# Two more PSUM buffers for the results of the layers, once the last head's scores are done

## The chip, the cores and the metric

The program runs on one core of one Trainium2 chip. The metric is the device time of one execution in microseconds (us): the median of three runs was 1069.62 us, the runs lying between 1068.02 and 1071.15 us.

## The reference

Attention with a decay, over 8 batches of 8 heads, 576 positions and 64 channels, and behind it two dense layers with a hard swish between them, over all 4608 tokens. Everything is float32.

```python
# q, k, v: (8, 8, 576, 64); f: (8, 8, 576)
scores = scale * q @ k.T
cum    = cumsum(log(clip(f, 1e-4, 1)))
scores = where(causal, -1e9, scores + cum[..., :, None] - cum[..., None, :])
attn   = exp(scores - max); attn /= attn.sum(-1) + 1e-9
x      = (attn @ v) -> (4608, 512)
h      = x @ w_in            # 512 -> 2048
g      = h * clip(h + 3, 0, 6) / 6
out    = g @ w_out           # 2048 -> 512
```

## The kernel before

**The work.** The 64 heads go through one after another (the loop over `VH`): scores by matmul into PSUM, maximum, exponential, weights times values, and the result `xT` laid down by transposing DMAs. As soon as all the heads of a batch are through, the two layers of that batch are appended to the list `units`, and `fill` hands pieces of them to TensorE (PE) between the pieces of the next heads. Every number is carried as a high and a low half in 16 bits, so each product in the layers is three matmuls (lines 785 to 787 and 832 to 834).

**Results of the layers.** A result is one tile of 128 partitions by 512 floats in PSUM, summed up by many matmuls and then taken out:

- `h_unit` (first layer, tile `ph`): 12 matmuls over 512 columns, traced in two blocks of six. Taken out by ScalarE (ACT, L791, `Relu` into `r`), VectorE (DVE, L794, the product, which reads `ph` a last time), ACT again (L795, high half into `gT`) and DVE again (L796, low half into `gT`). There are 16 of these for a batch.
- `out_unit` (second layer, tile `po`): 48 matmuls in eight blocks of six, which read all of `gT` and `w2`. Taken out by one ACT instruction (L838) into `o`, which a DMA writes to memory (L841). There are four for a batch.
- `rest_unit` (tile `ph_r`) and `out_unit` with the name `r…` (tile `po_r`): the same for the 64 tokens of each batch that fill no group of 512, for two batches together. `rest_unit` has 48 matmuls over 128 columns, in two blocks of 24; L817 (twice, ACT), L821 (DVE), L823 (ACT) and L824 (DVE) take it out, into `g_end` for the last pair of batches (the profile calls that place `vst`). Four `rest_unit`s, one last `out_unit`.

`gT` exists once: the first layer of a batch may overwrite a part of it only when all four `out_unit`s of the batch before have read that part. `r` has three buffers, `o` two.

**PSUM.** Four pools: `ps_s` (tag `S`, two buffers of 1024 floats, the heads' scores, `pn` and `ps`), `ps_m` (tag `mm`, two buffers of 512), `ps_t` (tag `tr`, one of 512) and `ps_a` (one, weights times values). `mm_tile` deals out the buffers of the layers: it counts the results in `turn`, and where `three` is set every third result takes `tr`, the others `mm`. So three buffers turn. In all 196 results are dealt out; 166 of them are asked for before the line `done(prev[0])` behind the loop, 30 after it: the last result of the first layer of batch 6 (counting from 0), four `out_unit`s of batch 6, and for batch 7 sixteen `h_unit`s, four `rest_unit`s, four `out_unit`s and the last `po_r`.

**What sets the order.** The order on each engine is laid down when the program is built, by a planner that walks through the program on estimated times. Of the instructions of an engine whose inputs and buffer are there, it takes the one with the lowest trace number, and it settles some matmuls ahead of the running one. Buffers of one tag go to their requests in traced order. `fill` traces each block inside `tc.high_priority(offset=-LOW_M)` with `LOW_M = 0`: its numbers start from where the outer trace stands, and the outer trace does not advance. Behind the heads nothing else is traced, only

```python
    while units:
        fill(1)
```

so there all blocks start from the same number, and only the place inside the block counts. Two results whose buffers and inputs are there therefore take turns in blocks of six, and a `rest_unit`, with its blocks of 24, gives way from its seventh matmul on to every block of six that is ready. On the chip each engine then runs its list strictly in this order.

Of the kernel before, what the change touches and what calls it, by code (L numbers as in the profile page):

```python
# [11 lines left out]
F32 = mybir.dt.float32  # L12
# [8 lines left out]
def kernel(  # L21
# [12 lines left out]
    NHEAD, D, S = qk.shape  # L34
# [5 lines left out]
    P = 128  # L40
# [6 lines left out]
    TT = 512  # L47
# [7 lines left out]
    ps_s = ctx.enter_context(tc.tile_pool(name="ps_s", bufs=2, space=bass.MemoryType.PSUM))  # L55
# [694 lines left out]
    def x_move(v):  # L750

        kind, n = VH[v]
        g = n if kind == "A" else n // 2
        b, cc = divmod(g, NPAIR)
        xhl = xpair[g][1]
        c0, c1, rest = {"A": (0, CA, None), "B": (CA, NCH - 1, NCH - 1), "F": (1, NCH, 0)}[kind]
        o = c0 - (1 if kind == "F" else 0)
        if rest is not None:
            nc.sync.dma_start_transpose(
                xT[2][:, cc, b // 2, :, 64 * (b % 2):64 * (b % 2) + 64],  # L760
                xhl[0:64, rest].rearrange("p a e -> p (a e)"),
            )
        nc.sync.dma_start_transpose(
            xT[b % 2][:, cc, o:o + c1 - c0].rearrange("p c a t -> p (c a) t"),
            xhl[:, c0:c1].rearrange("p c a e -> p (c a e)"),
        )


    turn = [0]

    def mm_tile(name, three):

        turn[0] += 1
        if three and turn[0] % 3 == 0:
            return ps_t.tile([P, TT], F32, tag="tr", name=name)
        return ps_m.tile([P, TT], F32, tag="mm", name=name)

    def h_unit(x, fc, c0, c1, b, three, name):

        nw = c1 - c0  # L780
        ph = mm_tile(f"ph_{name}_{fc}_{c0}", three)[:, :nw]
        fs_ = slice(fc * P, (fc + 1) * P)
        for cc in range(NCC):
            xh, xl = (x[:, cc, c0 // P:c1 // P, hl] for hl in range(2))
            nc.tensor.matmul(ph, w1[0][:, cc, fs_], xh, start=(cc == 0), stop=False)  # L785
            nc.tensor.matmul(ph, w1[0][:, cc, fs_], xl, start=False, stop=False)  # L786
            nc.tensor.matmul(ph, w1[1][:, cc, fs_], xh, start=False, stop=(cc == NCC - 1))  # L787
            if cc == 1 and nw == TT:
                yield H_COST
        r = p2.tile([P, TT], F32, tag="rt", name=f"r_{name}_{fc}_{c0}", bufs=3)[:, :nw]  # L790
        nc.scalar.activation(  # L791
            r, ph, AF.Relu, bias=bias_r, scale=scol(A1 + NG * b + fc * NG // NFC)
        )
        nc.vector.scalar_tensor_tensor(r, r, 6.0 * CG, ph, op0=ALU.min, op1=ALU.mult)  # L794
        nc.scalar.copy(gT[:, 0, fc, c0:c1], r)  # L795
        nc.vector.tensor_tensor(gT[:, 1, fc, c0:c1], r, gT[:, 0, fc, c0:c1], op=ALU.subtract)  # L796
        yield H_COST

    def rest_unit(k, j, g):

        n = NFC // NG
        ph = mm_tile(f"ph_r{k}_{j}", True)
        for i in range(n):
            fs_ = slice((n * j + i) * P, (n * j + i + 1) * P)
            dst = ph[:, i * P:(i + 1) * P]
            for cc in range(NCC):
                xh, xl = (xT[2][:, cc, k, hl] for hl in range(2))
                nc.tensor.matmul(dst, w1[0][:, cc, fs_], xh, start=(cc == 0), stop=False)  # L808
                nc.tensor.matmul(dst, w1[0][:, cc, fs_], xl, start=False, stop=False)
                nc.tensor.matmul(dst, w1[1][:, cc, fs_], xh, start=False, stop=(cc == NCC - 1))  # L810
            if i == n // 2 - 1:
                yield H_COST
        r = p2.tile([P, TT], F32, tag="rt", name=f"r_r{k}_{j}", bufs=3)
        r3, p3 = (t.rearrange("p (f t) -> p f t", t=P) for t in (r, ph))
        for i in range(2):
            o = slice(64 * i, 64 * i + 64)
            nc.scalar.activation(  # L817
                r3[:, :, o], p3[:, :, o], AF.Relu, bias=bias_r,
                scale=scol(A1 + NG * (2 * k + i) + j),
            )  # L820
        nc.vector.scalar_tensor_tensor(r, r, 6.0 * CG, ph, op0=ALU.min, op1=ALU.mult)  # L821
        hi, lo = (g[:, hl, n * j:n * (j + 1), 0:P] for hl in range(2))
        nc.scalar.copy(hi, r3)  # L823
        nc.vector.tensor_tensor(lo, r3, hi, op=ALU.subtract)  # L824
        yield H_COST

    def out_unit(s, col, rows, three, name, g=gT):

        po = mm_tile(f"po_{name}_{s}", three)
        ts_ = slice(s * P, (s + 1) * P)  # L830
        for fc in range(NFC):
            nc.tensor.matmul(po, g[:, 0, fc, ts_], w2[:, fc, 0, :], start=(fc == 0), stop=False)  # L832
            nc.tensor.matmul(po, g[:, 0, fc, ts_], w2[:, fc, 1, :], start=False, stop=False)  # L833
            nc.tensor.matmul(po, g[:, 1, fc, ts_], w2[:, fc, 0, :], start=False, stop=(fc == NFC - 1))  # L834
            if fc % 2 and fc < NFC - 1:
                yield 2.0 - H_COST
        o = p2.tile([P, DM], F32, tag="o", name=f"o_{name}_{s}")
        nc.scalar.activation(o, po, AF.Copy, scale=scol(col))  # L838
        p = 0
        for r0, r1 in rows:  # L840
            nc.sync.dma_start(out[r0:r1, :], o[p:p + r1 - r0])  # L841
            p += r1 - r0
        yield 2.0 - H_COST

    def moe_in(b, c0=0, c1=TT):

        for fc in range(NFC):
            j, new = divmod(fc, NFC // NG)
            if new == 0 and c0 == 0:
                while j not in w_in_done:  # L850
                    next(w_in_q, None)
                moe_scale_in(b, j)
            yield from h_unit(xT[b % 2], fc, c0, c1, b, b > 0 or c0 > 0, f"{b}")

    def moe_out(b, c0=0, c1=TT):

        if b == 0:
            for _ in wq:
                pass
        if c0 == 0:  # L860
            moe_scale_out(b)
        for s in range(c0 // P, c1 // P):
            r = S * b + (64 if b else 0) + s * P
            yield from out_unit(s, UO + b, [(r, r + P)], b > 0 or s * P >= QA, f"{b}")
# [4 lines left out]
    def rest_in(k, g):  # L869

        for j in range(NG):
            yield from rest_unit(k, j, g)

    def rest_out(k, g):

        b = 2 * k
        r = S - 64 if b == 0 else S * b
        yield from out_unit(
            0, UX + b + 1, [(r, r + 64), (S * (b + 1), S * (b + 1) + 64)], True, f"r{k}", g
        )  # L880
# [52 lines left out]
    def fill(k):  # L933
        credit[0] += k * rates[0]
        while credit[0] >= 1 and units:
            with tc.high_priority(offset=-LOW_M):
                r = next(units[0], 0)
            if r == 0:
                units.pop(0)
            else:  # L940
                credit[0] -= r
        credit[0] = min(credit[0], 1.0)

    def done(v):
        kind, n = VH[v]
        if kind == "A":
            if n == NPAIR - 1:
                units.append(moe_in(0, 0, QA))
                units.append(moe_out(0, 0, QA))
            return  # L950
        b, h = divmod(n, H)
        if h == H - 1:
            cut = QA if b == 0 else 0
            units.append(moe_in(b, cut, TT))
            if b == B - 1:
                units.append(rest_in(b // 2, g_end))
            units.append(moe_out(b, cut, TT))
            if b == B - 1:
                units.append(rest_out(b // 2, g_end))
            elif b % 2:  # L960
                units.append(rest_in(b // 2, gT))
                units.append(rest_out(b // 2, gT))

    prev = None
    pend_x = None
    vq = v_scale(0)
    for i, (kind, n) in enumerate(VH):
# [61 lines left out]
        prev = (i, ph)  # L1029
# [2 lines left out]
    fill(4)  # L1032
    x_move(prev[0])
    done(prev[0])
    while units:
        fill(1)

# [35 lines left out]
```

## Time and profile before

| | |
|---|---|
| median of 3 runs | 1069.62 us (1068.02 to 1071.15) |
| the profiled execution | 1067.75 us, of which the profile's span is 1065.7 us |
| PE busy | 1005.6 us (94%), 7650 matmuls |
| DVE, ACT, POOL busy | 714.6, 633.5, 439.4 us |
| chain that ended last | PE 81%, DVE 9%, ACT 4%, DMA 4%, issue 2% |
| mean granted PE clock | 0.988 |

A row of the timeline gives start and length in us, engine, line, operation, `out<-in`, the shape and how many are merged (`x3`); in brackets stands how long the engine had been idle and what released it. [...] A row of the table by stretches gives, for a stretch of the span, the busy time of each engine (and its instructions), then the granted PE clock as a share, the share of DMA and GB/s. The waits are listed as "engine line waited for: us in total, times, longest".

### The profile page before, as it was taken

What the parts mean: (1) busy time and instruction counts of PE and PEld (TensorE: products, weight loads), DVE (VectorE), ACT (ScalarE), POOL (GpSimd) and SP (SyncE); (2) the same over time, 40 slices, a digit from 0 to 9 for tenths busy, and PEclk for the clock granted to TensorE, in tenths of its full rate; (3) what the DMA queues carried; (4) which work ended last, traced back from release to release, by engine and by line L of the source; (5) the groups of instructions that cost most, each with busy time, mean ns of one, the idle gap of its engine ahead of it and who ended that gap; (6) DMA issues with size and microseconds to landing.
All of it is one profiled execution on the core that took longest, in us unless ns stands there. A gap on an engine that the chain in (4) does not pass through costs nothing.

```text
span 1065.7 us, 21332 instructions
## 1 busy us (share of the span) xinstructions
PE 1005.6 (94%) x7650; PEld 598.6 (56%) x7650; DVE 714.6 (67%) x1887; ACT 633.5 (59%) x1257; POOL 439.4 (41%) x641
## 2 busy tenths in 40 slices
PE   2799967899999999999999999999999999999897
PEld 2567844665555755555555755555555755444543
DVE  6878799886867678866885778847895677115300
ACT  5798667766864657656755657646764666125301
POOL 9635556435544445454553445545544430000000
PEclk9999989999999999999999999999999999999999
DMA  8875446936766675567565755566556544010000
GB/s 239 275 216 174 110 101 136 210 77 118 158 118 120 119 160 106 95 144 154 104 125 109 160 112 109 106 130 163 105 97 137 91 89 74 12 40 1 1 20 30
DMA packets 253717, 123.83 MB, mean 116 GB/s; under 512 B 225860, under 2 KB 227452, under 8 KB 253612
## 3 DMA queue, kind: packets, MB, share of 16 engines
q1 hardware_dynamic: 253612, 122.47, 53.2%
q8 instruction: 60, 0.98, 0.4%
q14 instruction: 45, 0.37, 0.1%
HBM read 47.93 MB, written 9.73 MB: 54 GB/s over the span
## 4 chain that ended last, share of the span: by engine, by line
PE 81%; DVE 9%; ACT 4%; DMA 4%; issue 2%; SPq 0%; POOL 0%; ACTq 0%; DVEq 0%; POOLq 0%
PE ph L785 10%; PE ph L786 10%; PE ph L787 10%; PE po L832 10%; PE po L834 10%; PE po L833 10%; PE pn L622 3%; PE pn L619 3%; DMA ring<-in_w_in_dram 2%; DVE pp L630 1%; PE pav L706 1%; PE pav L707 1%; PE pav L705 1%; PE po_r L834 1%; PE ph_r L808 1%
## 5 line engine op out<-in xcount | busy, mean ns | idle before, releaser
L642 ACT ACTIVATE pp<-pp,nb 128x192 f32<-128x192 f32 x280 | 138.4, 552 | 133.7 <-DVE nb L636 119.6
L785 PE MATMUL ph<-xT,w 128*128 128x512 f16 (+1 forms) x576 | 198.4, 358 | 3.6 <-ACT o L838 2.3
L659 DVE TENSOR_TENSOR ring<-pp,ring 128x128 f16<-128x128 f32 (+2 forms) x216 | 142.2, 671 | 83.5 <-ACT ring L656 77.8
L787 PE MATMUL ph<-xT,w 128*128 128x512 f16 (+1 forms) x576 | 197.9, 357 | 0.0
L786 PE MATMUL ph<-xT,w 128*128 128x512 f16 (+1 forms) x576 | 197.8, 357 | 0.0
L832 PE MATMUL po<-w,gT 128*128 128x512 f16 x512 | 189.5, 381 | 7.5 <-ACT w L284 3.5
L833 PE MATMUL po<-w,gT 128*128 128x512 f16 x512 | 192.1, 381 | 3.7 <-DVE w L295 3.7
L464 POOL TENSOR_TENSOR T<-ST,TQ 64x288 fp32r<-64x288 f32 (+2 forms) x136 | 112.0, 825 | 199.2 <-PE pn L622 153.0
L834 PE MATMUL po<-w,gT 128*128 128x512 f16 x512 | 191.7, 381 | 0.0
L630 DVE CUSTOM_DVE_ANT_0 pp<-pn,W 128x192 f32<-128x192 f32 x280 | 123.5, 483 | 32.1 <-PE pn L622 21.9
L794 DVE SCALAR_TENSOR_TENSOR r<-r,ph 128x512 f32<-128x512 f32 (+1 forms) x144 | 89.1, 620 | 68.1 <-ACT r L791 67.5
L619 PE MATMUL pn<-TK,TQ 68*128 68x192 f32 x336 | 125.9, 388 | 5.8 <-issue 5.7
L469 POOL TENSOR_TENSOR T<-ST,T 64x288 fp32r<-64x288 f32 (+1 forms) x136 | 125.5, 941 | 12.6 <-ACT T L462 7.9
L791 ACT ACTIVATE r<-ph,bias_r,SC 128x512 f32<-128x512 f32 (+1 forms) x144 | 103.8, 725 | 26.0 <-PE ph L787 22.8
L796 DVE TENSOR_TENSOR gT<-r,gT 128x512 f16<-128x512 f32 (+1 forms) x144 | 102.5, 714 | 23.5 <-ACT gT L795 21.8
L622 PE MATMUL pn<-T,T 128*128 128x192 f32 x336 | 116.0, 370 | 0.0
L656 ACT CAST ring<-pp 128x192 f16<-128x192 f32 x280 | 114.4, 450 | 0.2
L795 ACT CAST gT<-r 128x512 f16<-128x512 f32 (+1 forms) x144 | 81.1, 566 | 40.6 <-DVE r L794 40.2
L665 POOL TENSOR_TENSOR ring<-pp,ring 128x128 f16<-128x128 f32 x96 | 56.1, 584 | 104.0 <-ACT ring L656 84.4
L834 PEld LDWEIGHTS <-gT 128*128 128x128 f16 x560 | 54.7, 98 | 70.0 <-issue 10.3
L833 PEld LDWEIGHTS <-gT 128*128 128x128 f16 x560 | 54.9, 98 | 65.1 <-issue 10.2
L787 PEld LDWEIGHTS <-w 128*128 128x128 f16 x576 | 56.5, 98 | 57.0 <-issue 6.6
(159 smaller groups left out, 2036.3 us busy)
## 6 DMA issues: line engine op xcount, KB each, us to landing
ST<-in_qk_dram SPq DMA_DIRECT2D x64, 288.0 KB
ring<-in_w_out_dram SPq DMA_DIRECT2D x16, 512.0 KB
out_dram<-o SPq DMA_DIRECT2D x32, 256.0 KB
T<-TQ SPq DMA_DIRECT2D x56, 144.0 KB
vst<-in_vS_dram SPq DMA_DIRECT2D x7, 1040.0 KB
ring<-in_w_in_dram SPq DMA_DIRECT2D x9, 512.0 KB
w<-in_w_in_dram SPq DMA_DIRECT2D x7, 512.0 KB
vst<-in_vS_dram SPq DMA_DIRECT2D x14, 130.0 KB
```

The source lines that it names most:

```text
L469: nc.gpsimd.tensor_tensor(T1[j][0:D, a:e], s[D:, a:e], T1[j][D:, a:e].bitcast(F32), op=ALU.subtract)
L619: nc.tensor.matmul(dst, TQ[i][0:D + 4, qs], TK[i][0:D + 4, a:e], start=True, stop=False)
L622: nc.tensor.matmul(dst, T7[j][:, qs], T1[j][:, a:e], start=False, stop=True)
L630: nc.vector.tensor_tensor_reduce(pp[:r, w:w + kw], pn[:r, o:o + kw], W[:r, 4 * P + r - kw:4 * P + r], 1.0, -3.0e38, ALU.add, ALU.max, accu ...
L642: nc.scalar.activation(x_, x_, AF.Exp, bias=nb[:r, e0 + x:e0 + x + 1], scale=0.125)
L659: eng.tensor_tensor(hl[:r, a:a + c * P], pp[:r, at[c] + 64:at[c] + kw], hl[:r, h0[c] + 64:h0[c] + kw], op=ALU.subtract,)
L785: nc.tensor.matmul(ph, w1[0][:, cc, fs_], xh, start=(cc == 0), stop=False)
L786: nc.tensor.matmul(ph, w1[0][:, cc, fs_], xl, start=False, stop=False)
L787: nc.tensor.matmul(ph, w1[1][:, cc, fs_], xh, start=False, stop=(cc == NCC - 1))
L832: nc.tensor.matmul(po, g[:, 0, fc, ts_], w2[:, fc, 0, :], start=(fc == 0), stop=False)
L833: nc.tensor.matmul(po, g[:, 0, fc, ts_], w2[:, fc, 1, :], start=False, stop=False)
L834: nc.tensor.matmul(po, g[:, 1, fc, ts_], w2[:, fc, 0, :], start=False, stop=(fc == NFC - 1))
```

## The change

From the point where the last head is through, `mm_tile` gives every result with an odd count a buffer of `ps_s` (half of it is used), and the results with an even count go on as before: `tr` where the count can be divided by three, `mm` otherwise. Of the 30 results after that point, those with the counts 167, 169, … 195 go to `S`: 15 of them. Two buffers of `S`, two of `mm` and one of `tr` make five. No instruction is added or taken away.

```diff
     turn = [0]
+    heads_done = []
 
     def mm_tile(name, three):
 
         turn[0] += 1
+        if heads_done and turn[0] % 2:
+            return ps_s.tile([P, 1024], F32, tag="S", name=name)[:, :TT]
         if three and turn[0] % 3 == 0:
             return ps_t.tile([P, TT], F32, tag="tr", name=name)
         return ps_m.tile([P, TT], F32, tag="mm", name=name)
...
     x_move(prev[0])
     done(prev[0])
+    heads_done.append(prev[0])
     while units:
         fill(1)
```

## The prediction

> **What bounds the kernel now.** First the page's parts 1 and 2, to see which engine fills the span and whether the part that the change touches (the end, behind the last head) is different.
>
> ```profile
> PE 1005.6 (94%) x7650; PEld 598.6 (56%) x7650; DVE 714.6 (67%) x1887; ACT 633.5 (59%) x1257; POOL 439.4 (41%) x641
> ...
> PE   2799967899999999999999999999999999999897
> ```
>
> TensorE is the bound from the ninth slice on, and there only the third-last and the last slice fall short. A buffer more can do one thing alone: take away time in which PE waits for a buffer. So the next view is the table by stretches, cut at the places where PE stood, and the list of PE's waits from 903 us on.
>
> ```profile
> core 0: us, PE busy (x) PEld busy (x) DVE busy (x) ACT busy (x) POOL busy (x), PEclk, DMA share, GB/s
> 885.00:903.00 18.00, 18.00 (x146) 9.42 (x145) 12.70 (x31) 11.82 (x22) 1.63 (x3) 1.00 0.39 77
> 903.00:944.00 41.00, 40.22 (x201) 18.34 (x197) 4.98 (x9) 5.54 (x9) 0.00 (x0) 1.00 0.09 27
> 944.00:991.00 47.00, 47.00 (x220) 21.27 (x218) 20.08 (x30) 21.40 (x31) 0.00 (x0) 1.00 0.02 6
> ...
> 999.00:1002.00 3.00, 0.26 (x5) 0.14 (x3) 0.79 (x2) 2.75 (x7) 0.00 (x0) 1.00 0.00 0
> 1002.00:1054.00 52.00, 52.00 (x276) 24.91 (x275) 2.90 (x5) 4.38 (x8) 0.00 (x0) 1.00 0.06 21
> 1054.00:1057.00 3.00, 0.52 (x2) 0.11 (x2) 1.23 (x2) 1.64 (x3) 0.00 (x0) 1.00 0.00 0
> 1057.00:1061.10 4.10, 3.86 (x11) 1.14 (x10) 0.15 (x1) 0.08 (x1) 0.00 (x0) 0.61 0.00 0
> ```
>
> ```profile
> PE po L832 <- DVE r_r L821: 2.7, 1, 2.7
> PE po_r L832 <- ACT vst L823: 2.5, 1, 2.5
> PE po L832 <- ACT o L838: 0.8, 1, 0.8
> ```
>
> PE is full in 885 to 903, in all of the first layer of batch 7 (944 to 991: 47.00 of 47.00 us with three buffers) and from 1002 to 1054. It stands at three places, and behind the third the granted clock is 0.61. These places are the whole stake. The timeline shows what each is.
>
> ```profile
> 938.05 0.38 PE L834 MATMUL po<-w,gT 128*128 128x512 f16 x1
> 939.20 0.38 PE L832 MATMUL po<-w,gT 128*128 128x512 f16 x1 [0.78 <-ACT o L838]
> ...
> 998.87 0.33 PE L810 MATMUL ph_r<-xT,w 128*128 128x128 f16 x3
> 1001.95 0.38 PE L832 MATMUL po<-w,gT 128*128 128x512 f16 x1 [2.75 <-DVE r_r L821]
> ...
> 1053.78 0.22 PE L810 MATMUL ph_r<-xT,w 128*128 128x128 f16 x1
> 1056.48 0.39 PE L832 MATMUL po_r<-w,vst 128*128 128x512 f16 x1 [2.49 <-ACT vst L823]
> 1056.71 0.38 PE L833 MATMUL po_r<-w,vst 128*128 128x512 f16 x1
> 1057.21 0.39 PE L834 MATMUL po_r<-w,vst 128*128 128x512 f16 x1
> ...
> 1057.87 0.56 PE L834 MATMUL po_r<-w,vst 128*128 128x512 f16 x1
> 1058.22 0.63 PE L832 MATMUL po_r<-w,vst 128*128 128x512 f16 x1
> ...
> 1060.35 0.63 PE L834 MATMUL po_r<-w,vst 128*128 128x512 f16 x1
> 1061.02 0.69 ACT L838 ACTIVATE o_r<-po_r,SC 128x512 f32<-128x512 f32 x1 [4.59 <-PE po_r L834]
> ```
>
> For scale, how a result of the first layer is taken out while PE goes on:
>
> ```profile
> 985.60 0.38 PE L787 MATMUL ph<-xT,w 128*128 128x512 f16 x1
> 986.08 0.78 ACT L791 ACTIVATE r<-ph,bias_r,SC 128x512 f32<-128x512 f32 x1 [0.44 <-PE ph L787]
> 986.89 0.69 DVE L794 SCALAR_TENSOR_TENSOR r<-r,ph 128x512 f32<-128x512 f32 x1 [0.53 <-ACT r L791]
> ...
> 988.19 0.38 PE L787 MATMUL ph<-xT,w 128*128 128x512 f16 x1
> ```
>
> The last matmuls of two results stand 2.59 us apart, so one of the 12 takes 0.216 us; the buffer is given back at 986.89 + 0.69 = 987.58, that is 1.98 us after its last matmul began, 0.6 us before the last matmul of the next result begins. Three buffers are enough here.
>
> **The stakes, step by step.** No instruction is added or removed, and no transfer is. What changes is which of the 30 last results wait for which.
>
> (a) End of the second layer of batch 6: from 938.05 to 939.20 are 1.15 us where 0.22 would do: 0.93 us. The fourth `po` waits for the first one's buffer; three `po` had gone round together and ended together.
>
> (b) The three `rest_unit`s that hold the three buffers end together (998.87, three merged, the last at 998.98), and the next matmul waits until ACT and DVE have given one back: 1001.95 - 998.98 less one step of 0.055 (998.87 to 998.98 are two) = 2.91 us.
>
> (c) The fourth `rest_unit` gets its buffer late, and because its blocks are 24 long it gives way to every `po` until the end. Its last matmul is at 1053.78, and only `po_r`, which needs what it yields, is left: 1056.48 - 1053.78 - 0.055 = 2.65 us, and 1057.21 - 1056.71 - 0.22 = 0.28 us for the low half.
>
> (d) From 1057.87 to 1060.35 there are six steps in 2.48 us where 1.30 would do, and the last matmul takes 0.63 where 0.38 is usual: 1.18 + 0.25 = 1.43 us. That is the half clock behind stall (c), and it goes with it.
>
> Together 0.93 + 2.91 + 2.65 + 0.28 + 1.43 = 8.20 us. Without any of it PE's last matmul would end at 1060.98 - 8.20 = 1052.8; the change cannot gain more.
>
> **What the change does with each.** It can start early: the last reader of a score buffer is DVE's L630,
>
> ```profile
> 891.69 0.08 DVE L630 DVE_READ_ACCUMULATOR2_ANT MF<- 128x1 f32 x1
> ```
>
> 10 us before the first result that could use it runs, so no head waits for a layer. PE has no idle time there, so results pulled forward only change places.
>
> (a) goes: with a `po` each on `tr`, `S`, `mm`, `S`, all four of batch 6 run at once, and the other `mm` buffer is there for the first layer of batch 7. I take 0.93 us; bounds 0 and 0.93.
>
> (c) and (d) go: the counts 188 to 191 put the four `rest_unit`s on `mm`, `S`, `mm`, `S`, so the fourth has its buffer before the second layer starts and no longer ends alone behind everything. 2.65 + 0.28 + 1.43 = 4.36 us; the cover is 41 us of second layer (4 x 48 x 0.216) behind it.
>
> (b) stays, at the same price: the four `rest_unit`s now sit on both `mm` and both `S`, and the only result of the second layer that has a buffer meanwhile is count 192, on `tr`. By the rule of the blocks that one goes first, and the rest units fill up behind it, in turns, and end nearly together. Then PE again has nothing whose buffer is free until ACT and DVE have given one back. Bounds: 0, if the turns let one of them end earlier or the `tr` result last longer; 2.91, the row above. I take 2.91, since the same three instructions ended the wait there.
>
> The end itself gets worse. Before, the last result stands alone. With four buffers free behind the rest units, the last four results (three `po` and `po_r`) go round in blocks of six and end close together, and `o` has two buffers:
>
> ```profile
> 938.46 1.26 ACT L838 ACTIVATE o<-po,SC 128x512 f32<-128x512 f32 x2 [27.56 <-PE po L834]
> 941.34 0.69 ACT L838 ACTIVATE o<-po,SC 128x512 f32<-128x512 f32 x1 [1.61 <-DMA out_dram<-o]
> ```
>
> Two that end together cost the second 0.63 us; a third waits for the first one's DMA and starts 2.88 us after it; a fourth 2.88 + 0.63 = 3.51. So 0 to 3.51 us. Two of the four may have ended a turn before (six matmuls are 1.3 us), so I take the middle between the second and the third, (0.63 + 2.88) / 2 = 1.75. SP only issues these DMAs; nothing else stands in its queue.
>
> Sum: 8.20 - 2.91 - 1.75 = 3.5 us. The profiled execution took 1067.75 us (2.05 beside its span) and lies 1.87 under the median of 1069.62; the difference is taken off the median: **1066.1 us**. Its own range goes from no pile-up at the end (gain 5.3: 1064.3) to four ends at once (gain 1.8: 1067.8).
>
> [...] Stall (b) left the clock at 1.00, stall (c), not longer, was followed by 0.61. [...]
>
> **The rivals.**
>
> - All stalls go. If a rest unit ends before the others, or the `tr` result outlasts them, (b) goes too, and 8.20 less one doubled end of 0.63 gives 7.6 us: 1062.0. For it: (b) hangs on several units ending within 0.1 us, and five buffers leave more to choose from. Against it: they ended so before.
> - (b) stays and halves the clock behind it: 3.5 - 1.43 = 2.1 us gained, 1067.5. For it: one of the two long stalls did that. Against it: the very same stall (b) did not.
> - Slower. Buffers of a tag, and those of `r` and `o`, go out in traced order, so a result that finishes early keeps its PSUM until the earlier ones are taken out: ACT's 27.56 us idle and two L838 back to back show it, and the even counts now run ahead of the odd ones. If in the first layer of batch 7 PE runs dry at each turn, it waits from the end of the last matmul (985.60 + 0.38) to the release at 987.58: 1.6 us. Five such waits eat up the 8.20; all eight odd counts of the first layer cost 12.8 us: 1074.2. Against it: 47.00 of 47.00 us busy with fewer buffers.
> - Nothing happens: the planner lays the results out so that the same waits stand, or others of the same size; 1069.6. For it: all the order behind the heads is re-planned, so that 3 to 5 us of new waits at other places are possible.
>
> [...] I give it 0.02, inside the slower case.
>
> **How the numbers follow.** Chances: the forecast 0.42, all stalls gone 0.22, half clock 0.16, nothing 0.10, slower 0.10. The three runs lie 3.1 us apart, so 0.3% (3.2 us) is about what can be told from no change. The forecast's own range (gain 1.8 to 5.3) lies for six tenths above 3.2 us: 0.25; with nearly all of the first rival and a fifth of the second that is 0.50 faster. Slower is the third rival, nearly all of it: 0.09. The rest, 0.41, is within 0.3%. The range goes from the first rival, 1062.0, to nothing with half a us of scatter, 1070.2; the slower case and the lower half of the first rival's scatter stay out.
>
> **What would show it.** In the profile after: no wait of `po` for L838 around 938 us (a); one wait of 2.5 to 3 us of a `po` for L821, somewhere between 1000 and 1015 us (b); no wait of `po_r` for L823, and the clock at 1.00 in the last matmuls (c, d); the last matmul ends at 1055 to 1056 us; two or more L838 back to back at the end, one of them behind a DMA. I am wrong if PE shows new waits inside the first layer of batch 7, if the rest units do not end together, or if `rest_unit`s again end last.

## The result and the profile after

The changed kernel took 1061.20 us (median, 1060.59 to 1062.22), the kernel before 1069.76 beside it: ratio 0.9919, 95% interval 0.9902 to 0.9936, a gain of 8.6 us where 3.5 were forecast. Measured a second time (e9 below) it took 1061.52 against 1069.05: 0.9935 (0.9922 to 0.9947).

The profiled execution of the changed kernel took 1060.59 us (span 1058.5). Its lines are three higher than before: 788 to 790 for `ph`, 811 to 813 for `ph_r`, 835 to 837 for `po`, 820 and 824 for the taking out of a `rest_unit`, 841 for `o`. Of the page, the share of PE and its slices:

```profile
PE 1006.1 (95%) x7650; PEld 599.4 (57%) x7650; DVE 714.1 (67%) x1887; ACT 633.0 (60%) x1257; POOL 440.0 (42%) x641
...
PE   2799978899999999999999999999999999999998
```

PE has the same work (1006.1 us; before 1005.6). The third-last slice, an 8 before, is full. The table by stretches says the same finely; the last row ends shortly behind PE's last matmul:

```profile
core 0: us, PE busy (x) PEld busy (x) DVE busy (x) ACT busy (x) POOL busy (x), PEclk, DMA share, GB/s
...
903.00:944.00 41.00, 41.00 (x226) 19.25 (x225) 5.92 (x11) 5.58 (x8) 0.00 (x0) 1.00 0.04 8
944.00:991.00 47.00, 47.00 (x252) 22.63 (x250) 16.38 (x25) 19.01 (x29) 0.00 (x0) 1.00 0.06 23
991.00:1011.00 20.00, 20.00 (x190) 12.92 (x188) 5.93 (x10) 6.27 (x12) 0.00 (x0) 1.00 0.04 15
1011.00:1050.00 39.00, 39.00 (x201) 18.38 (x199) 4.37 (x7) 6.15 (x12) 0.00 (x0) 1.00 0.04 14
1050.00:1054.00 4.00, 3.82 (x18) 1.55 (x16) 0.00 (x0) 0.59 (x2) 0.00 (x0) 1.00 0.17 66
```

From 903 us to the end of its last matmul at 1053.82 PE never stands, and the clock is 1.00 in every row. All three stalls are gone, (b) too.

How much of the gain lies behind the heads is read from the last score matmul, the same instruction in both traces, first before, then after:

```profile
889.43 0.55 PE L622 MATMUL pn<-T,T 128*128 128x448 f32 x1
```

```profile
890.50 0.55 PE L622 MATMUL pn<-T,T 128*128 128x448 f32 x1
```

From its start to the end of the span are 176.25 us before and 168.03 after: 8.23 us less. (The heads ran 1.07 us later in this execution, so the spans differ by 7.2 only.) That is the sum of all the stalls, 8.20 us, which the prediction had as the most that could be gained. This length, "from the last score matmul", is what the experiments are compared by; it leaves out the scatter of the heads.

Why (b) is gone is seen where the rest units end. The timeline after, PE first, then ACT and DVE:

```profile
1007.97 0.27 PE L813 MATMUL ph_r<-xT,w 128*128 128x128 f16 x2
...
1011.04 0.38 PE L835 MATMUL po<-w,gT 128*128 128x512 f16 x1
...
1053.44 0.38 PE L837 MATMUL po_r<-w,vst 128*128 128x512 f16 x1
```

```profile
1008.29 1.02 ACT L820 ACTIVATE r_r<-ph_r,bias_r,SC 128x256 f32<-128x256 f32 x2 [1.77 <-PE ph_r L813]
1010.96 1.02 ACT L820 ACTIVATE r_r<-ph_r,bias_r,SC 128x256 f32<-128x256 f32 x2 [0.28 <-PE ph_r L813]
...
1032.07 1.27 ACT L841 ACTIVATE o<-po,SC 128x512 f32<-128x512 f32 x2 [18.72 <-PE po L837]
1033.23 1.94 ACT L820 ACTIVATE r_r<-ph_r,bias_r,SC 128x256 f32<-128x256 f32 x4
...
1049.75 0.69 ACT L841 ACTIVATE o<-po,SC 128x512 f32<-128x512 f32 x1 [13.07 <-PE po L837]
1053.85 0.69 ACT L841 ACTIVATE o_r<-po_r,SC 128x512 f32<-128x512 f32 x1 [3.41 <-PE po_r L837]
```

```profile
1009.34 0.69 DVE L824 SCALAR_TENSOR_TENSOR r_r<-r_r,ph_r 128x512 f32<-128x512 f32 x1 [12.02 <-ACT r_r L820]
```

L820 runs twice for each `rest_unit`. Here it comes in three places: the first unit ends at 1007.97, the second at 1010.7, two at 1033. The first one's buffer is free when DVE has read it, at 1009.34 + 0.69 = 1010.03. Until 1011.04 PE has over fifty matmuls of the other rest units to do, so the next `po` starts without a gap. And the end is no pile-up: `o` leaves at 1032 (two), at 1049.75 and at 1053.85, each with its buffer free.

### The profile page after: what moved, and what is told of

The parts are those of the page before. It is cut to its first block, busy times and chain, and to the rows that moved or that the text cites. A ratio compares the mean times of both kernels' runs of the same rounds, so it can differ in the third digit from the quotient of the medians.

```text
span 1058.5 us, 21322 instructions
## 1 busy us (share of the span) xinstructions
PE 1006.1 (95%) x7650; PEld 599.4 (57%) x7650; DVE 714.1 (67%) x1887; ACT 633.0 (60%) x1257; POOL 440.0 (42%) x641
## 4 chain that ended last, share of the span: by engine, by line
PE 80%; DVE 9%; DMA 4%; ACT 4%; issue 2%; SPq 0%; POOL 0%; ACTq 0%; DVEq 0%; POOLq 0%
PE ph L788 10%; PE po L835 10%; PE po L837 10%; PE po L836 10%; PE ph L789 10%; PE ph L790 10%; PE pn L622 3%; PE pn L619 3%; PE pav L706 1%; PE pav L707 1%; PE ph_r L811 1%; PE pav L705 1%; PE ph_r L812 1%; PE ph_r L813 1%; PE po_r L835 1%
```

## The experiments

The question is why the stall (b) and the pile-up, both forecast, did not come. The theory: what costs is several results that end together, and it is the order of the blocks that decides on this; more buffers help only as far as they change that order. The rival: five buffers as such do it. "Length" in the table is the time from the last score matmul to the end in the profiled execution (before 176.25); "saved" is the difference to that. Both are of one execution each, and the one of before contains the 1.43 us of half clock, (d). Behind the same stall (c) the clock of e1 and e11 is 1.00, so the author takes it that (d) is not in every execution of before; no second trace of before shows it. It would explain that e7, e11 and e12 save some 2 us of length, while the intervals of their medians contain 1. The kernel before ran beside each group (medians 1069.11 for e1, e2, e3, e7; 1069.05 for e4, e6, e8, e9; 1068.69 for e11, e12; 1068.54 for e13, e14).

| kernel | median us | ratio (95%) | length us | saved |
|---|---|---|---|---|
| e9: the change again | 1061.52 | 0.9935 (0.9922 to 0.9947) | 168.02 | 8.23 |
| e1: S for the counts up to 171 | 1067.75 | 0.9989 (0.9971 to 1.0006) | 174.19 | 2.07 |
| e2: S for the counts 189 and 191 | 1065.36 | 0.9966 (0.9952 to 0.9981) | 170.98 | 5.28 |
| e3: before, last rest units in sixes | 1066.87 | 0.9982 (0.9970 to 0.9994) | 174.13 | 2.13 |
| e4: before, rest units ahead of the first layer | 1063.92 | 0.9958 (0.9945 to 0.9971) | 172.17 | 4.09 |
| e6: the change on the even counts | 1063.28 | 0.9954 (0.9939 to 0.9968) | 170.49 | 5.76 |
| e7: the change, four rest units in one block each | 1068.72 | 0.9994 (0.9980 to 1.0009) | 174.09 | 2.16 |
| e8: the change, last result in halves | 1061.43 | 0.9936 (0.9920 to 0.9952) | 168.22 | 8.03 |
| e11: S for the counts 167 to 187 | 1067.47 | 0.9994 (0.9982 to 1.0006) | 173.89 | 2.36 |
| e12: S for the counts 189 to 195 | 1068.48 | 1.0000 (0.9985 to 1.0014) | 174.27 | 1.99 |
| e13: the change, first rest unit in one block | 1068.32 | 0.9998 (0.9988 to 1.0009) | 175.96 | 0.29 |
| e14: the change, the other three in one block | 1066.18 | 0.9978 (0.9964 to 0.9993) | 171.55 | 4.70 |

**The parts of the change: e1 and e2.**

```diff
-        if heads_done and turn[0] % 2:
+        if heads_done and turn[0] % 2 and turn[0] <= 171:   # e1
+        if heads_done and turn[0] in (189, 191):            # e2
```

> Score buffers only for the counts 167 to 171 (the end of batch 6). Theory (the gain is the sum of the stalls a to d and of nothing else): only stall (a), 0.93 us, goes; the waits of 2.7 us for L821 and 2.5 us for L823 and the half clock at the end stay: 1068.8 us, no difference that can be told. Rival (more buffers make the first layer of batch 7 run better, and the stalls further on go with that): half of the gain or more, 1065.5 us or less.

> Score buffers only for two of the four last rest units (counts 189 and 191), everything else as before. Theory: the fourth rest unit no longer ends alone, so (c) and (d) go, 4.36 us; whether (b) goes depends on whether the rest units end together: if together, a wait of 2.9 us of a po for L821 stays and the time is about 1065 us; if not, about 1062 us. Rival (all five buffers have to turn through both layers): the gain is under 2 us.

PE's list of waits behind the heads in e1; in e2 the first of these two lines stands alone:

```profile
PE po L835 <- DVE r_r L824: 2.7, 1, 2.7
PE po_r L835 <- ACT vst L826: 2.5, 1, 2.5
```

e1 loses (a), and behind the same stall (c) its clock stays at 1.00: 0.93 + 1.43, less a new wait of 0.14 us with its restart, is its 2.07. e2 keeps (b) alone, as late as 1026 us, and saves 5.28 us, what 8.20 - 2.91 gives: two score buffers under two rest units take out (c) and (d), and (a) too. These two units need not wait for batch 7's first layer: their inputs and buffers are there, and 26 of their matmuls run between 885 and 930 us, in the middle of batch 6, where before has none. The four `po` of batch 6 then leave one by one (ACT takes them out at 937.40, 940.21, 941.76 and 955.96), and none has to wait. (b) stands, so it needs more than that.

**Same buffers, other blocks: e7.** The change as it is, but each last `rest_unit` is one block of 48 matmuls, not two of 24.

```diff
-            if i == n // 2 - 1:
+            if i == n // 2 - 1 and k < 3:
```

> The five buffers of the changed kernel, but each of the last rest units is traced as one block of 48 matmuls, so that all four take turns matmul by matmul and end together. Theory (stall b went because one rest unit ended ahead of the other three, whose matmuls then covered its taking out): a wait of 2.5 to 3 us of a po for L824 is back, some 2.9 us more than the changed kernel: 1064.1 us. Rival (five buffers as such remove the wait): no such wait, 1061.2 us.

Its waits, and ACT's timeline:

```profile
PE po L835 <- DVE r_r L824: 2.6, 1, 2.6
```

```profile
1012.61 2.84 ACT L820 ACTIVATE r_r<-ph_r,bias_r,SC 128x256 f32<-128x256 f32 x6 [5.79 <-PE ph_r L813]
...
1056.74 1.26 ACT L841 ACTIVATE o<-po,SC 128x512 f32<-128x512 f32 x2 [37.19 <-PE po L837]
1059.60 0.69 ACT L841 ACTIVATE o<-po,SC 128x512 f32<-128x512 f32 x1 [1.60 <-DMA out_dram<-o]
1060.22 0.69 ACT L841 ACTIVATE o_r<-po_r,SC 128x512 f32<-128x512 f32 x1
```

Five buffers, and the gain is gone but for 2.16 us. Six L820 stand together: three rest units end at once, stall (b) is back, and the last four results end together. Counted from the last score matmul, PE's last matmul ends 2.79 us later than with the change, and from there to the end are 7.98 instead of 4.71 us: 3.27 more. These are the two terms of the prediction, at about its prices (2.91; up to 3.51), in a kernel where the rest units do end together. The median, 1068.72, lies above the 1064.1 expected, which had no pile-up in it.

**The two halves of the dealing: e11 and e12.**

```diff
+        if heads_done and turn[0] % 2 and turn[0] <= 187:   # e11
+        if heads_done and turn[0] % 2 and turn[0] >= 189:   # e12
```

> The changed kernel with the score buffers for the odd counts 167 to 187 alone: the last result of batch 6's first layer, its second layer and the first layer of batch 7 have five buffers, the four rest units and the last second layer have three as before. Theory (stall (b) goes only where a rest unit holds an early buffer and the others still have work when it is taken out; that takes free buffers both in front of and under the rest units): (a) goes, one stall of 2.6 to 2.9 us with a po waiting for L824 stands, and the last rest unit ends alone in front of po_r, 2.5 to 2.9 us again: gain 0.9 to 2.4 us, 1066.7 to 1068.2. Rival (the buffers in front of the rest units are what takes (b) out): no wait for L824, only the one in front of po_r: gain 3.8 to 5.3 us, 1063.8 to 1065.3.

> The other half: score buffers for the odd counts 189 to 195 alone, two rest units and two results of the last second layer; before them three buffers turn. Theory: the rest units get their buffers late and together, so stall (b) stands (2.6 to 2.9 us, a po waiting for L824), as does (a), 0.9 us, if the count 171 is what took it out; (c) goes: gain about 4.4 us less up to 3.5 us if the last results end together, 1064.8 to 1068. Rival (the score buffers under the rest units and behind them are all that the change needs): (b) gone as well, gain 7.3 us, 1061.9.

The waits of e11, and ACT's timeline of e12 (whose only wait is the first of these lines, at 1015.4 us):

```profile
PE po L835 <- DVE r_r L824: 2.7, 1, 2.7
PE po_r L835 <- ACT vst L826: 2.5, 1, 2.5
```

```profile
1012.66 2.84 ACT L820 ACTIVATE r_r<-ph_r,bias_r,SC 128x256 f32<-128x256 f32 x6 [3.50 <-PE ph_r L813]
```

Both rivals fall. The halves save 2.36 (again 0.93 + 1.43) and 1.99 us, the whole 8.23. All three contain the 1.43 us of half clock that the execution of before had and these three had not (1.00 behind the stalls of e11 and e12, and up to the last matmul with the change); without it they are 0.93, 0.56 and 6.80. The medians say the same: 1.2 and 0.2 us for the halves, 7.5 to 8.6 for the whole. (At 1068.48, e12 even lies above the 1064.8 to 1068 expected.) e12 is what the prediction described: the rest units are taken out together behind one stall, none stands in front of `po_r`, and at the end come two, one and one `o` as in e7. From the change it differs only in what is in front of the rest units: three buffers there, not five. That this matters is what the prediction did not see; it had looked at the first layer and found PE full. (a) went in e12 too, against the expectation; up to 930 us PE runs as many matmuls of rest units there as in e2.

e12 and e2 differ in two results alone, the counts 193 and 195: two of the last `po` have score buffers in e12 and not in e2. Both have the same stall, and PE's last matmul comes 166.22 us behind the last score matmul in both. But from there to the end are 8.05 us in e12 and 4.76 in e2, where `po_r` stands alone at the end. So the pile-up, 3.29 us, is what more buffers behind rest units that end together cost.

**One matmul: e13 and e14.** The order that the planner laid down for PE shows what the early buffers do. This extract is from the built programs, not from a trace. A number in brackets says how many of its 48 matmuls a result has behind it; "rest 0" is the first of the four last rest units, and `po` 0 to 3 are batch 7's.

```
change  rest 0 (47) | first layer ends | po 0 (48) | rest 1, 2, 3 in turns (23) | rest 0 (48) | rest 1, 3 (47) | rest 1 (48) | po 2 ...
e13     rest 0 (47) | first layer ends | po 0 (48) | rest 1, 2, 3 in turns (23), then each (47) | rest 2, 1, 3, 0 (48) | po 2 ...
e14     rest 0 (47) | first layer ends | po 0 (48) | rest 1, 2, 3 in turns (23) | rest 0 (48) | rest 1, 2, 3 in turns (41) | po 2 (48) | rest 2, 3, 1 (48) ...
e12     rest 1, 3 (48) | first layer ends | po 0 (48) | rest 0, 2 in turns (23), then each (47) | rest 0, 2 (48) | po 2 ...
```

The last matmul of rest 0 is the 24th of its second block, so it comes when the others have the 24th of their first block in front of them: there they still have half their work. In e12 it is rest 1 and rest 3 that are through early, on score buffers that nobody else uses in the first layer; but results are taken out in traced order, so they hold their PSUM until rest 0 is out. The trace of e12 agrees: 96 matmuls of `ph_r`, two whole units, run before 991 us, and ACT's first L820 comes at 1012.66. e13 and e14 change the blocks alone:

```diff
-            if i == n // 2 - 1:
+            if i == n // 2 - 1 and not (k == 3 and j == 0):   # e13
+            if i == n // 2 - 1 and not (k == 3 and j > 0):    # e14
```

> The change, but the first of the last pair's four rest units (and it alone) is one block of 48 matmuls instead of two of 24. By the order laid down, 47 of its 48 matmuls still run inside the first layer, as in the change; the last one now counts as the 48th of a block and comes behind the other three rest units, not in the middle of them. Theory (the stall goes because the first rest unit, whose taking out all the others wait for, ends while the others still have work): moving this one matmul is enough to bring stall (b) back, 2.6 to 2.9 us of a po waiting for L824 near 1015 us, six L820 in a row, and the pile-up at the end with it: 2.0 to 2.5 us saved from the last score matmul, 1067 to 1069 us. Rival (early buffers are what counts, and three units in two blocks each leave enough cover): no long wait, 1061.5 us.

> The reverse: the first rest unit keeps its two blocks of 24, the other three are one block of 48 each. Theory: the first one ends as in the change, its L820 stands alone near 1008.3 us and the next po (on its buffer) starts without a wait near 1011; but the other three now end together behind that po, so a stall of 2.6 to 2.9 us stands some ten us later (48 matmuls of 0.216), near 1022 us, and with it some pile-up at the end: 2 to 5.4 us saved, 1064 to 1068.5 us. Rival (the lead of the first one is all that is needed): no wait, 1061.5 us.

The waits and ACT's timeline, e13 first:

```profile
PE po L835 <- DVE r_r L824: 2.8, 1, 2.8
```

```profile
1012.52 2.85 ACT L820 ACTIVATE r_r<-ph_r,bias_r,SC 128x256 f32<-128x256 f32 x6 [5.96 <-PE ph_r L813]
```

```profile
PE po_r L835 <- DVE r_r L824: 2.7, 1, 2.7
```

```profile
1007.86 1.02 ACT L820 ACTIVATE r_r<-ph_r,bias_r,SC 128x256 f32<-128x256 f32 x2 [1.77 <-PE ph_r L813]
...
1022.35 2.85 ACT L820 ACTIVATE r_r<-ph_r,bias_r,SC 128x256 f32<-128x256 f32 x6 [12.09 <-PE ph_r L813]
```

The stalls came as the theory had them. One matmul of rest 0 put behind the others, and nearly the whole gain is gone: 0.29 us saved, and 2.0 without the 1.7 us that the half clock behind the stall cost here (reckoned below). With rest 0 as in the change and the others in one block, its `po` starts without a wait; the stall comes behind that one, at 1025 us, when the three end together, with `po_r` in the place of a `po`, and two `o` end together at the end: 4.70 us saved.

**Three buffers, another order: e3 and e4.** e3 hands over the last rest units in blocks of six, like everything else; e4 traces them ahead of the first layer of batch 7.

```diff
# e3
+                if k == 3 and cc % 2 and not (cc == NCC - 1 and i in (n // 2 - 1, n - 1)):
+                    yield H_COST / 4
             if i == n // 2 - 1:
-                yield H_COST
+                yield H_COST / 4 if k == 3 else H_COST
# e4
+            if k == 3:
+                moe_scale_in(2 * k + 1, j)
             yield from rest_unit(k, j, g)
...
-            units.append(moe_in(b, cut, TT))
             if b == B - 1:
                 units.append(rest_in(b // 2, g_end))
+            units.append(moe_in(b, cut, TT))
```

> Three buffers as before, but the last four rest units are traced in blocks of 6 matmuls in place of 24, so that they no longer give way to every po. Theory: (c) and (d) go without any buffer, (a) and (b) stay: 4.36 us less, 1065.3 us. Rival (the fourth rest unit is late because it lacks a buffer, and only a buffer mends that): as before, 1069.7 us.

> Three buffers as before; only the four rest units of the last pair are traced ahead of the first layer of batch 7 and not behind it. Theory (the order in which the rest units end is what costs, the number of buffers only as far as it sets that order): they get buffers early, none ends last in front of po_r, so (c) and (d) go without any further buffer, 4.36 us, to about 1065.3 us; stall (a), 0.93, stays, and one stall of about 2.9 us where a buffer has to be given back with nothing to cover it, since only three turn. Rival (five buffers are what does it): with three, two stalls of 2.5 us or more stand as before, and the time stays at 1068 to 1069.7. Second rival (any early rest unit takes all long stalls out): only (a) stays, 1062.4 us.

The waits of e3 (its lines are two higher than before), then of e4 (lines as before):

```profile
PE po L834 <- DVE r_r L823: 2.7, 1, 2.7
PE po L834 <- ACT o L840: 0.8, 1, 0.8
```

```profile
PE ph L785 <- DVE r L794: 2.0, 1, 2.0
PE po L832 <- ACT o L838: 1.6, 2, 0.8
```

In e3 stall (c) goes without any further buffer, but the gain is 2.13 us where 4.36 were expected. Of the difference 0.64 us are two `o` that end together (so much longer than before from the last matmul to the end); the rest, 1.6 us, is about the 1.7 us that the clock cost, reckoned below. e4 saves 4.09 us on three buffers, half of the whole gain, by order alone: neither (b) nor (c) is in its list. It keeps (a), has another of the same kind, and a wait of 2.0 us in the first layer, where the rest units now hold buffers; expected was one stall of 2.9 us.

**Another assignment: e6.** The even counts take the score buffers.

```diff
-        if heads_done and turn[0] % 2:
+        if heads_done and turn[0] % 2 == 0:
```

> The change with the other half: every even count on a score buffer, not every odd one. Five buffers turn as in the change, but which result sits where, and so which rest unit is early, is another. Theory (order): no stall of 2.5 us need come back, as two rest units still sit on score buffers, but other results end together; up to three stalls of 0.5 to 0.95 us like (a), so 1061.2 to 1063.8 us, and PE waits between 0 and 2.5 us in all. Rival 1 (the number of buffers alone does it): no wait at all, as in the change, 1061.2. Rival 2 (the change hit a lucky assignment): stall (b) back with 2.6 to 2.9 us, or the end pile-up of 2.9 to 3.3 us that the kernel with rest units in one block showed: 1064 to 1067.5.

```profile
PE ph L788 <- ACT o L841: 0.8, 1, 0.8
PE po_r L835 <- ACT o L841: 0.8, 1, 0.8
PE po L835 <- DVE r_r L824: 0.4, 1, 0.4
```

Five buffers, no long stall, three short ones of 2.0 us together; its length exceeds that of the change by 2.46. "The number of buffers alone does it" falls here too, and the long stall of the second rival is not there either: the assignment made is worth some 2 us.

**The way behind the last matmul: e8 and e9.** With PE full to the end, the 4.7 us behind it are what is left of this stage.

```diff
-        nc.scalar.activation(o, po, AF.Copy, scale=scol(col))
+        last = len(rows) == 2 and rows[0][0] >= NT // 2 + S * 2
+        if last:
+            nc.scalar.activation(o[:, 0:DM // 2], po[:, 0:DM // 2], AF.Copy, scale=scol(col))
+            nc.vector.tensor_scalar(o[:, DM // 2:], po[:, DM // 2:], scol(col), None, op0=ALU.mult)
...
+            eng = nc.scalar if last and i else nc.sync
+            eng.dma_start(out[r0:r1, :], o[p:p + r1 - r0])
```

> The change, and beside it a shorter way from the last matmul to the end, which is 4.7 us there: ACT takes out the left half of the last result and DVE the right half, instead of ACT both in 0.69 us, and the second of its two transfers is issued on ACT's queue, where SP issued both in 1.35 us. Theory (the last step is a chain of take-out, issue and landing): some 0.3 us from the halves and 0.67 us from the issue, 0.7 to 1.0 us less than the changed kernel, 1060.2 to 1060.5. Rival (the landing of the transfer sets the end, whoever issues it, and two small halves cost what one whole does): within 0.3 us of the changed kernel.

> The changed kernel once more, as the yardstick of the three beside it. If the first gain was the order and not chance: about 8 us under the kernel before, no wait of PE behind the heads, 168.0 us from the last matmul of the heads to the end. If part of it was chance of one chip or one execution: a ratio nearer to 0.996 than to 0.992, or a wait of 2.5 us or more in the second layer of batch 7.

The end of e8 in the timelines of ACT, DVE and SP, and SP's of the changed kernel:

```profile
1053.74 0.47 ACT L843 ACTIVATE o_r<-po_r,SC 128x256 f32<-128x256 f32 x1 [3.41 <-PE po_r L837]
...
1054.76 0.57 ACTq L850 DMA_DIRECT2D out_dram<-o_r  x1
```

```profile
1054.25 0.48 DVE L844 TENSOR_SCALAR o_r<-po_r,SC 128x256 f32<-128x256 f32 x1 [16.96 <-ACT o_r L843]
```

```profile
1054.76 0.49 SPq L850 DMA_DIRECT2D out_dram<-o_r  x1
```

```profile
1054.57 1.35 SPq L844 DMA_DIRECT2D out_dram<-o_r  x2
```

Nothing is gained (1061.43 against 1061.52). DVE began when ACT was done: 0.47 + 0.48 one after the other, longer than the 0.69 of one piece; both read `po_r` and write the tile `o_r`; whether one of these is the reason is open. And the two issues side by side end 0.59 us sooner, yet from the first issue to the end are 3.8 us (1058.6 - 1054.76) where the changed kernel has 3.9 (1058.5 - 1054.57). So the rival holds: the end moved with the first issue, and the time that the second took was covered. No version tried beats the change.

## Why the prediction was wrong

- **(a) goes, 0.93: right**, though not for the reason given alone: batch 6's own buffers do it (e1, e11), but (a) also went in e2 and e12, where two rest units on score buffers run inside batch 6 and its `po` end one by one.
- **(c) goes, 2.65 + 0.28: right.** With score buffers under two rest units (e2, e12, the change) the wait for `vst` is gone; in e1 and e11, without them, it stands at 2.5 us. e3 and e4 show that the order of blocks can do it too, as the prediction's cause said (blocks of 24 that give way).
- **(d), 1.43, counted as bound to (c): not bound to it.** e1 and e11 have the same stall (c), 2.5 us, and a clock of 1.00 behind it. It was part of the profiled execution of before, so it counts in the 8.23 us; whether other executions of before have it was not shown.
- **(b) stays, 2.91: the step that failed.** "The rest units fill up behind it, in turns, and end nearly together" took the four for equals at the start. The table by stretches, for `ph_r` alone, shows what it missed, before and after:

```profile
930.00:991.00 61.00, 0.00 (x1) 1.00 0.05 18
```

```profile
930.00:991.00 61.00, 3.11 (x44) 1.00 0.05 18
```

  Before, one `ph_r` matmul runs before 991 us; after, 44 recorded ones. With five buffers in the first layer rest 0 gets its own inside it and is a block ahead when the others begin; so it ends in the middle of their work, 3 us of which cover the 2.06 us that taking it out needs. A lead alone is not enough. e13 and e7 leave it as it is (by the order laid down 47 of the 48 matmuls still run inside the first layer) and put only rest 0's last matmul behind those of the others; e11 has a part of the lead (27 recorded matmuls before 991 us) and ends together all the same; e12 gives the lead to the wrong units. In all four the forecast's stall is back, at 2.6 to 2.8 us. That the rest units do not end together was among the prediction's own signs of being wrong.
- **The pile-up at the end, 1.75: the second failed term, from the same step.** It is 3.27 us in e7, about the same in e12 and e13 (3.3), and 0 with the change, because rest units that end apart send the four last results on their way apart. Its reason as forecast, four free buffers behind rest units that end together, is borne out by e2, which has such rest units but fewer buffers behind them, and no pile-up.
- **The sum:** the forecast's gain of 3.54 and the two failed terms, 2.91 + 1.75, are 8.20; measured behind the heads are 8.23. PE's last matmul ends at 1053.82, before the 1055 to 1056 forecast. The rival "all stalls go" (1062.0) named the condition, "if a rest unit ends before the others"; it got the smaller chance because the trace of before has no such case.
- **The slower rival** did not come: 47.00 of 47.00 us busy in the first layer of batch 7. Its mechanism, a result that ends early but keeps its PSUM until the earlier ones are taken out, is what e12 runs into. For the 0.02 that the prediction gives inside this case no run shows a ground: in that layer (944 to 991 us) the clock is 1.00 with three buffers and with five.

## What to carry to other kernels

Ask of a further buffer not only who waits for it now, but whose start it moves forward: here most of its worth (7.5 to 8.6 us by the medians, against 1.4 for its two halves apart) came from one result that began early, was first in the order of taking out, and so ended apart from its like. Where several long results share buffers, stagger their ends; results that end together cost a stall of 2.6 to 2.8 us here, with three buffers and with five, and four at the end with two output buffers 3.3 us. Prices read from the trace held: in the list of waits the stall was 2.7 us before, and 2.6 to 2.8 wherever it came again (2.91 when reckoned from the starts of the matmuls, which there are 0.22 us long and start 0.055 us apart). What has to be worked out anew for the changed kernel is the order that calls for them.

## What the hardware showed

The half clock had the same length, 3.41 to 3.42 us, all three times that it was seen behind a stall, and not every stall brought it. The granted clock behind stall (c) of before, then behind the long stall of e3 and of e13, by stretches:

```profile
1057.50:1058.00 0.50, 0.50 (x4) 0.94 0.00 0
1058.00:1061.00 3.00, 2.98 (x8) 0.50 0.00 0
1061.00:1061.50 0.50, 0.00 (x0) 0.65 0.00 0
```

```profile
1001.50:1002.00 0.50, 0.00 (x0) 0.93 0.00 0
1002.00:1005.00 3.00, 2.98 (x8) 0.50 0.00 0
1005.00:1005.50 0.50, 0.50 (x3) 0.66 0.00 0
```

```profile
1016.00:1016.50 0.50, 0.50 (x4) 0.69 0.00 0
1016.50:1019.50 3.00, 3.00 (x9) 0.50 0.00 0
1019.50:1020.00 0.50, 0.50 (x4) 0.89 0.00 0
```

Taking the mixed slices apart into 1.00 and 0.50 (0.94 over half a us is 0.06 us of half clock), they last 3.41, 3.41 and 3.42 us. In e3 the half clock begins where the stall ends, in e13 1.0 us later, in before 1.5 us. By this reckoning e3 and e13, where PE is busy in 2.98 and 3.00 of the 3.00 us at 0.50, lose half of it, 1.7 us each. The long stalls of before, e1, e2, e3, e7 and e11 to e14 are twelve, of 2.5 to 2.8 us; these three alone were followed by it, behind the other nine the rows show 1.00. The same stall (c) in e1, behind which PE starts again at 1057.91, left the clock at 1.00:

```profile
1058.50:1061.00 2.50, 2.35 (x11) 1.00 0.00 0
```

The length of a stall does not tell them apart: in the list of waits the three that were followed by half clock have 2.5 (before), 2.7 (e3) and 2.8 us (e13), the nine others 2.5 to 2.7. Which stalls are hit no run here shows.
